# Gated GeGLU on one core: six units begin with the products that need no operand sums

## The chip, the cores and the metric

The kernel runs on one core of a Trainium2 chip. The metric is the device time of one execution in microseconds (us), as a median over runs. The core has a matrix engine (TensorE, PE in the profile), three elementwise engines (VectorE or DVE, ScalarE or ACT, GpSimd or POOL), a queue engine that issues the transfers here (SyncE or SP), and 16 DMA engines.

## What is computed

```python
# x (1, 2048, 1024), w_gate and w_up (1024, 3584), w_down (3584, 1024), all bf16
g = einsum("bsd,df->bsf", x, w_gate)
u = einsum("bsd,df->bsf", x, w_up)
h = gelu_tanh(g) * u
out = einsum("bsf,fd->bsd", h, w_down)
```

## The kernel before

All three products are done by the Strassen-Winograd scheme: a 2 by 2 block product takes seven block products instead of eight, at the price of sums of blocks, which the other engines make. The rows of x are taken in two passes of 1024, each as two chunks of 512 rows. A pass holds its rows transposed in two tiles `xT[0]` and `xT[1]`, each of eight K blocks of 128.

In the up projection a *unit* is 256 columns of w_gate and of w_up: two column blocks of 128, by two K halves of four blocks, against two row chunks. Its seven products, each four matmuls for gate and four for up, are P1 and P2, which use the bf16 blocks as loaded, and P6, P5, P3, P7, P4, which use sums in fp32r. The row sums `t1` to `t4` and the cast `tb` are made once per pass from `xT`; the weight sums `s1` to `s4` and the cast `sa` are made for each unit from its weight tile `w`. The first row chunk is `lo`/`hi` of `xT[0]`, the second of `xT[1]`.

P1 is copied out of PSUM by ACT (`snap`, the copy `p1`); P1 + P2 gives block (0,0) of the output. P6 is accumulated by the matrix engine onto P1 in the same PSUM bank; that sum is copied out as `u2`, and then P3 and later P4 are accumulated in the same bank again. P5 goes to another pair of banks, is copied out as `p5`, and P7 is accumulated on it.

The order on SP, DVE, POOL and PE, and in these sections on ACT, is the order in which the program is written (`manual_schedule`); nothing is reordered. All loads are issued by SP, one after the other.

The start is special. Four DMAs load the first 512 rows of x (`load_x`, L435), and PE transposes them, 32 blocks of 128 x 128, through four PSUM banks (`turn`, L444; seven and two dummy matmuls in `keep_warm`, L500, precede and separate them). The second 512 rows come transposed by DMA (`transposing`, L452), eight of them. The first 256 columns of the weights, unit 0, are done without the scheme: `plain` (L478) makes 32 bf16 matmuls for each row chunk, `finish` (L493) the gelu and the product with up. Between the two stand P1 and P2 of unit 1 (`raw_products`, L189). Then the units from 1 to 13 follow, called from L594 on. In an odd unit, ahead of P4, the raw products P1 and P2 of the next two units are done (`ahead_of_p4`, L584). `aside` (L576) makes t4 after P6 of unit 1 and loads the weights of the unit after next; `prepare` (L560) has POOL make the weight sums of the next unit. From unit 2 on, `keep_part` (L265) makes sums of w_down for the down projection in the same banks.

Tiles with the tag "k" (t, s, p1, u2, p5, g and others) share 52 slots of 2 KB per partition; weight tiles share three buffers of 8 KB.

Of the kernel before, what the change touches and what calls it, by code (L numbers as in the profile page):

```python
# [10 lines left out]
def kernel(  # L11
# [23 lines left out]
    nc = tc.nc  # L35
# [23 lines left out]
    NWARM = 7  # L59
    SLOTS = 52  # L60
# [44 lines left out]
    def snap(ps, name):  # L105
        t = slot([P, N], f32, name)
        nc.scalar.copy(out=t, in_=ps)  # L107
        return t

# [7 lines left out]
    def load_w(u, queue=nc.sync):  # L117
        f0 = u * 2 * P
        w = wpool.tile([P, 2, NKB, 2 * P], bf16, name="w")
        for i, src in enumerate((w_gate, w_up)):  # L120
            queue.dma_start(
                out=w[:, i],
                in_=src[:, f0 : f0 + 2 * P].rearrange("(ko ki) f -> ki ko f", ki=P),
            )
        return w

# [22 lines left out]
    def sums_s(w, eng):  # L149
        GU = range(2)  # L150
        sh = [P, KH, P]
        a11, a21 = [[w[:, i, :KH, h : h + P] for i in GU] for h in (0, P)]
        a12, a22 = [[w[:, i, KH:, h : h + P] for i in GU] for h in (0, P)]
        return Sums(
            how={
                "s1": lambda q, GU=GU: [new(eng, a21[i], a22[i], ADD, "s1", sh) for i in GU],
                "s2": lambda q: [new(eng, q["s1"][i], a11[i], SUB, "s2", sh) for i in GU],
                "s3": lambda q: [new(eng, a11[i], a21[i], SUB, "s3", sh) for i in GU],
                "s4": lambda q: [new(eng, a12[i], q["s2"][i], SUB, "s4", sh) for i in GU],
                "sa": lambda q: [cast(a22[i], "sa", sh) for i in GU],  # L160
            }
        )
# [26 lines left out]
    def raw_products(e, c, xT, w):  # L189
        for i in range(2):  # L190
            product(e[i], w[:, i, :KH, :P], [xT[0][:, k, :] for k in range(KH)], True)
        p1 = [snap(e[i], "p1") for i in range(2)]
        for i in range(2):
            b21 = [xT[0][:, KH + k, :] for k in range(KH)]
            product(c[i], w[:, i, KH:, :P], b21, True)
        return p1
# [6 lines left out]
    def finish_raw(u, c, p1):  # L203
        g, up = add(c, p1)
        times(2 * u, 0, gelu(g), up)

    def unit(u, banks, s, t, late, after_p5, aside, keep, ahead_of_p4, behind_p4):
        GU = range(2)
        e, c, d = banks
        aside(-2)  # L210
        g, up = late() if late else (None, None)
        aside(-1)
        for i in GU:
            product(e[i], s["s2"][i], t["t2"], False)
        aside(0)
        keep(0, c[0])
        u2 = [snap(e[i], "u2") for i in GU]
        if late:
            g = gelu(g)
        c11 = g, up  # L220
        keep(1, c[0])
        keep(2, c[1])
        c = d
        for i in GU:
            product(c[i], s["s1"][i], t["t1"], True)
        p5 = [snap(c[i], "p5") for i in GU]
# [3 lines left out]
        g, up = new(dve, e[0], p5[0], ADD, "sum", dtype=f32), banks[1][not late]  # L230
        dve(up, e[1], p5[1], ADD)
        if late:
            times(2 * u, 0, *c11)
        for i in GU:
            product(c[i], s["s4"][i], t["tb"], False)
        times(2 * u + 1, 1, gelu(g), up)
        aside(1)
        g, up = add(c, u2)
        times(2 * u, 1, gelu(g), up)
# [4 lines left out]
        times(2 * u + 1, 0, gelu(e[0]), e[1])  # L244
# [190 lines left out]
    def load_x(c):  # L435
        t = []
        for i in range(NS):
            xn = slot([P, Dm], bf16, "xn")
            r0 = c * N + i * P
            nc.sync.dma_start(out=xn, in_=x2[r0 : r0 + P, :])  # L440
            t.append(xn)
        return t

    def turn(xT, xn, c, i):  # L444
        tp = bank[4 + i].bitcast(bf16).rearrange("p (k r) -> p k r", k=NKB)
        for ko in range(NKB):
            nc.tensor.transpose(tp[:, ko, :], xn[i][:, ko * P : (ko + 1) * P], ident)  # L447
        for ks in (range(NKB),) if i < NS - 1 else (range(KH), range(KH, NKB)):
            ks = slice(ks.start, ks.stop)
            (on_act if i == 1 else on_dve)(out=xT[c][:, ks, i * P : (i + 1) * P], in_=tp[:, ks])  # L450
# [6 lines left out]
    def load_wf(queue, k0, k1):  # L457
        for i, src in enumerate((w_gate, w_up)):
            got = queue.dma_start(
                out=wf[:, i, k0:k1],  # L460
                in_=src[k0 * P : k1 * P, 0 : 2 * P].rearrange(
                    "(ko ki) f -> ki ko f", ki=P
                ),
            )
            if queue is not nc.sync:
                tc.keep_in_program_order(got)

    xT = new_x()
    xn0 = load_x(0)
    wf = wpool.tile([P, 2, NKB, 2 * P], bf16, name="w")  # L470
    for k0, k1 in ((0, 2), (2, 5), (5, NKB)):
        load_wf(nc.sync, k0, k1)
    w = load_w(1)
    for ko in range(NKB):
        transposing(xT, 1, ko, N)
    ahead = load_w(2)

    def plain(ps, c, kos, parts=1):  # L478
        n = N // parts
        for k in range(kos.start, kos.stop, 2):  # L480
            for part in range(parts):
                cols = slice(part * n, (part + 1) * n)
                for p, (j, i) in zip(ps, [(j, i) for j in range(2) for i in range(2)]):
                    for ko in (k, k + 1):
                        matmul(
                            p[:, cols],
                            wf[:, i, ko, j * P : (j + 1) * P],
                            xT[c][:, ko, cols],
                            ko == 0 and part == 0,
                            ko == NKB - 1,  # L490
                        )

    def finish(ps, c):  # L493
        for j in range(2):
            times(j, c, gelu(ps[2 * j]), ps[2 * j + 1])

    on_dve, on_act = nc.vector.tensor_copy, nc.scalar.copy
    s, t = sums_s(w, dve), sums_t(xT)
    with tc.manual_schedule(engines={ENG.Activation}):
        def keep_warm(n, cols):  # L500
            for _ in range(n):
                nc.tensor.matmul(
                    bank[3][:, :cols], lhsT=warm[:, :P], rhs=warm[:, :cols], start=True, stop=True
                )

        keep_warm(NWARM, N)
        for i in range(NS):
            if i == 2:
                keep_warm(2, 2 * P)
            turn(xT, xn0, 0, i)  # L510
        plain(bank[0:4], 0, range(0, 2), parts=2)
        plain(bank[0:4], 0, range(2, NKB))
        s["s3"] = sums_s(w, pool)["how"]["s3"](s)
        s["s1"] = s["how"]["s1"](s, range(1))
        finish(bank[0:4], 0)
        s["s1"] += s["how"]["s1"](s, range(1, 2))
        nxt = {"p1": raw_products(odd, cc, xT, w)}
        s.make("sa", "s2", "s4")
        t.make("t1")

    seen = xpool.tile([P, 1], f32, name="seen")

    def rest_of_0(part):
        if part == 0:
            plain(bank[4:8], 1, range(NKB))
            t.make("t2", "tb")
        else:
            t3 = t["how"]["t3"](t, range(0, 2))
            finish(bank[4:8], 1)
            t["t3"] = t3 + t["how"]["t3"](t, range(2, KH))  # L530
# [6 lines left out]
    E, K, C, F = odd, cc, dd, even  # L537

    def loaded(u):
        if u not in ws:  # L540
            ws[u] = load_w(u)
        return ws[u]

    def raw_of(u, e):
        p1 = raw_products(e, K, xT, loaded(u))
        return lambda: finish_raw(u, K, p1)

    for ip in range(NPASS):
        with tc.manual_schedule(engines={ENG.Activation}):
            if ip == 0:  # L550
                ws = {1: w, 2: ahead}
                late = lambda: add(cc, nxt["p1"])
            else:
                raw_of(0, F)()
                raw_of(1, C)()
            for u in range(1 if ip == 0 else 0, NU):
                js = making(u) if ip == 0 else []
                first = (ip, u) == (0, 1)

                def prepare():  # L560
                    if first:
                        pool_behind(t["t4"][-1])
                    if u + 1 < NU:
                        nxt["s"] = make_s(loaded(u + 1), pool)
# [11 lines left out]
                def aside(part):  # L576
                    if first and part < 0:
                        rest_of_0(part + 2)
                    if part == 0 and u + 2 < NU:
                        loaded(u + 2)  # L580
                    if part == 0 and "t4" not in t:
                        t.make("t4")

                def ahead_of_p4():  # L584
                    if u % 2 and u + 1 < NU:
# [7 lines left out]
                if u % 2 and not first:  # L593
# [3 lines left out]
                    u, banks, s, t, late if first else None, prepare, aside, keep,  # L597
                    ahead_of_p4, behind_p4,
# [6 lines left out]
        def more(step):  # L605
# [9 lines left out]
            if step == 50:  # L615
                ws.clear()
                ws.update({n: load_w(n) for n in range(2)})
            if step == 58:
                got["s"] = make_s(ws[0], dve)
# [36 lines left out]
```

## Time and profile before

| | |
|---|---|
| median of 3 runs | 540.39 us (540.03 to 541.08) |
| profiled execution: span from first to last instruction | 538.8 us |
| median of the runs less the span | 1.6 us |
| PE busy | 534.1 us, 99% of the span, 2409 matmuls |
| DVE, ACT, POOL busy | 341.5, 261.4, 238.5 us |
| moved by DMA | 93.29 MB, mean 173 GB/s |
| granted PE clock (mean) | 1.000 |

The profile gives the span of its own execution and no separate device time for it; the runs' median is 1.6 us above it. The chain that ended last is the list of what released what, followed back from the last instruction: 98% of it is PE. A timeline line has the start, the time from the first start to the last end of the merged instructions, the engine, the line of the program, the operation with its tiles, and how often. In a merged line the recorded ends overlap the next start, so a rate is read from start to next start. Start times are counted from the first instruction.

### The profile page before, as it was taken

The numbers are of one execution on the slowest core, as the hardware profiler recorded it, in microseconds if no ns is written. First come the engines' busy times: TensorE is split into PE (matmuls) and PEld (weight loads), VectorE is DVE, ScalarE is ACT, GpSimd is POOL, SyncE is SP. The second block draws the span as 40 slices with busy tenths as digits, with TensorE's granted clock in tenths as the row PEclk, the third lists the DMA queues.
The fourth block names the chain that finished last, engine by engine and source line by source line (L and its number), as shares of the span: only waits on it lengthen the run. The fifth ranks groups of instructions, "written<-read, shape, count | busy, mean of one in ns | idle before, by whom it ended". The sixth has DMA issues, their size and how long they took to land.

```text
span 538.8 us, 7447 instructions
## 1 busy us (share of the span) xinstructions
PE 534.1 (99%) x2409; PEld 381.2 (71%) x2409; DVE 341.5 (63%) x524; ACT 261.4 (49%) x463; POOL 238.5 (44%) x215
## 2 busy tenths in 40 slices
PE   8999999999999999999999999999999999999997
PEld 5568686867677746888867677676868685488886
DVE  2986766767676894694955455555554649676730
ACT  2556675766666410255355555555555551114431
POOL 1179966677773500000097767676766600000000
DMA  9675656749472999989872223242420049573751
GB/s 243 157 185 168 185 176 175 220 133 260 131 235 72 381 366 297 307 192 296 238 195 80 78 80 88 70 118 63 133 71 9 2 147 390 184 236 96 237 181 51
DMA packets 108198, 93.29 MB, mean 173 GB/s; under 512 B 17280, under 2 KB 93056, under 8 KB 108160
## 3 DMA queue, kind: packets, MB, share of 16 engines
q1 hardware_dynamic: 108160, 92.82, 59.4%
q8 instruction: 19, 0.31, 0.3%
q14 instruction: 19, 0.16, 0.1%
HBM read 74.45 MB, written 15.20 MB: 166 GB/s over the span
## 4 chain that ended last, share of the span: by engine, by line
PE 98%; DMA 1%; SPq 0%; ACT 0%; issue 0%
PE bank L111 98%; DMA xn<-in_x_dram 1%; SPq L440 0%; PE bank L447 0%; ACT st L412 0%
## 5 line engine op out<-in xcount | busy, mean ns | idle before, releaser
L93 POOL TENSOR_TENSOR s<-w 128x512 fp32r<-128x512 bf16 x102 | 119.2, 1189 | 163.2 <-DVE t L90 86.0
L111 PE MATMUL bank<-t,s 128*128 128x512 f32 x648 | 151.7, 390 | 0.0
L111 PEld LDWEIGHTS bank<-t,s 128*128 128x128 f32 x648 | 121.6, 188 | 25.5
L111 PE MATMUL bank<-xT,w 128*128 128x512 bf16 (+1 forms) x504 | 109.7, 376 | 0.0
L107 ACT COPY p<-bank 128x512 f32<-128x512 f32 x124 | 69.9, 590 | 45.4 <-PE bank L111 44.9
L111 PEld LDWEIGHTS <-w 128*128 128x128 bf16 x504 | 48.1, 98 | 58.1 <-issue 3.4
L90 DVE TENSOR_TENSOR hT<-g,bank 128x512 bf16<-128x512 f32 x112 | 76.8, 687 | 17.5 <-PE bank L111 4.5
L90 DVE TENSOR_TENSOR sum<-bank,p 128x512 f32<-128x512 f32 x54 | 37.3, 691 | 79.5 <-PE bank L111 78.4
L179 ACT ACTIVATE g<-sum 128x512 f32<-128x512 f32 x81 | 51.4, 635 | 74.5 <-DVE sum L90 74.2
L111 PE MATMUL bank<-q 128*128 128x512 f32 x240 | 58.9, 389 | 0.0
L93 POOL TENSOR_TENSOR s<-w,s 128x512 fp32r<-128x512 bf16 x50 | 57.7, 1176 | 0.0
L93 POOL TENSOR_TENSOR s<-s,w 128x512 fp32r<-128x512 f32 x50 | 57.2, 1165 | 0.0
L111 PE MATMUL bank<-t,sa 128*128 128x512 f32 x216 | 55.9, 401 | 0.0
L111 PE MATMUL bank<-tb,s 128*128 128x512 f32 x216 | 53.3, 389 | 0.0
L107 ACT COPY u<-bank 128x512 f32<-128x512 f32 x62 | 35.5, 589 | 33.5 <-PE bank L111 33.2
L111 PEld LDWEIGHTS bank<-q 128*128 128x128 f32 x240 | 45.0, 188 | 9.4
L111 PE MATMUL bank<-raw,hT 128*128 128x512 bf16 x224 | 48.7, 379 | 0.0
L102 ACT CAST tb<-raw 128x512 fp32r<-128x512 bf16 x28 | 17.3, 626 | 62.1 <-PE bank L111 27.6
L111 PEld LDWEIGHTS bank<-t,sa 128*128 128x128 f32 x216 | 40.6, 188 | 9.5
L111 PEld LDWEIGHTS bank<-tb,s 128*128 128x128 f32 x216 | 40.5, 188 | 8.4
L90 DVE TENSOR_TENSOR bank<-bank,p 128x512 f32<-128x512 f32 x54 | 37.7, 699 | 8.8 <-PE bank L111 6.2
L90 DVE TENSOR_TENSOR q<-hT 128x512 fp32r<-128x512 bf16 x56 | 38.4, 685 | 4.3 <-PE bank L111 4.3
(44 smaller groups left out, 442.1 us busy)
## 6 DMA issues: line engine op xcount, KB each, us to landing
raw<-in_w_down_dram SPq DMA_DIRECT2D x76, 256.0 KB, 5.0
q<-td SPq DMA_DIRECT2D x60, 256.0 KB, 5.1
w<-in_w_gate_dram SPq DMA_DIRECT2D x27, 512.0 KB, 5.9
w<-in_w_up_dram SPq DMA_DIRECT2D x27, 512.0 KB, 7.0
td<-m SPq DMA_DIRECT2D x12, 768.0 KB, 4.5
w<-td SPq DMA_DIRECT2D x6, 1024.0 KB, 10.0
out_dram<-st SPq DMA_DIRECT2D x32, 128.0 KB, 1.7
td<-w SPq DMA_DIRECT2D x2, 768.0 KB, 6.2
```

The costliest lines, as they stand in the source:

```text
L90: nc.vector.tensor_tensor(out=out, in0=a, in1=b, op=op)
L93: nc.gpsimd.tensor_tensor(out=out, in0=a, in1=b, op=op)
L102: nc.scalar.copy(out=t, in_=src)
L107: nc.scalar.copy(out=t, in_=ps)
L111: nc.tensor.matmul(ps, lhsT=lhs, rhs=rhs, start=start, stop=stop, skip_group_check=True)
L179: nc.scalar.activation(g, src, ACT.Gelu_apprx_tanh)
```

## The change

Unit 0 becomes a unit like the others, and units 0 to 5 begin with P1 and P2 (`early_p1`, `early_p2`), two units at a time in four bank pairs, before any of their sums is needed. Their P1 copies are kept: eight in slots, four in parts of `hT` that are not yet written. The other five products follow for each unit in turn. Since P1 is then no longer in the bank, P6 starts the bank afresh and DVE adds the kept P1 to it before ACT copies `u2`. The copies `u2` and `p5` of the first pass go into `xT[1]`, which is no longer read by then.

Column blocks are paired differently in units 0 to 5, so that P1 and P2 of two units need one weight tile only; weight tiles 3 to 5 are loaded into a part of `hT`. The first x chunk is loaded in two K halves of two DMAs each, between pieces of the first weight tile; PE transposes one half before P1 of units 0 and 1 and the other between their P1 and P2. From unit 6 on, and in the second pass, the work is as before.

The core of the diff (the new `load_w` takes a number, a tile and a K range; `turn` takes a half; `blocks_of` picks the column blocks):

```diff
-    def unit(u, banks, s, t, late, after_p5, aside, keep, ahead_of_p4, behind_p4):
+    def unit(fbs, banks, s, t, p1, spare, after_p5, aside, keep, ahead_of_p4, behind_p4):
...
         for i in GU:
-            product(e[i], s["s2"][i], t["t2"], False)
-        aside(0)
+            product(e[i], s["s2"][i], t["t2"], p1 is not None)
+        if p1:
+            for i in GU:
+                dve(e[i], e[i], p1[i], ADD)
+        aside()
         keep(0, c[0])
-        u2 = [snap(e[i], "u2") for i in GU]
...
+        u2 = [snap(e[i], "u2", spare[i]) for i in GU]
...
+    load_x(0)
+    load_w(0, wa[0], 0, 2)
+    load_w(0, wa[0], 2, 4)
+    load_x(1)
+    load_w(0, wa[0], 4, 6)
+    load_w(0, wa[0], 6, 8)
+    load_w(2, wa[2])
+    for ko in range(KH):
+        transposing(xT, 1, ko, N)
+    load_w(4, wa[4])
+    load_w(1, wa[1])
+    for ko in range(KH, NKB):
+        transposing(xT, 1, ko, N)
+    load_w(3, wa[3])
+    load_w(5, wa[5])
+    early = [blocks_of(wa[u // 2 * 2], wa[u // 2 * 2 + 1], u % 2) for u in range(R)]
...
+        for us in (((2, C), (3, F)), ((4, E), (5, K))):
+            for u, ps in us:
+                for i in range(2):
+                    early_p1(u, ps, i, range(KH))
+                early_snap(u, ps)
+            if us[0][0] == 2:
+                t.make("t1")
+                s_pool.make("s3")
+                s["s3"] = s_pool["s3"]
+                s.make("s1", "s2")
+            else:
+                t.make("t2", "t3", "tb")
+            for u, ps in us:
+                for i in range(2):
+                    early_p2(u, ps, i, range(KH))
+                early_c11(u, ps)
+        s.make("s4", "sa")
+        t.make("t4")
+        pool_behind(t["t3"][-1])
+        nxt = {"s": make_s(early[1], pool)}
```

`early_c11` is the gelu and the product with up for block (0,0) of a unit: one ACT and one DVE instruction.

## The prediction

> **What bounds the kernel now.** I read the page first (span, slices, chain), then the chain in order of time, then the timelines of PE, DVE and SP over the first 45 us, where the change lies. The page:
>
> ```profile
> span 538.8 us, 7447 instructions
> PE   8999999999999999999999999999999999999997
> DVE  2986766767676894694955455555554649676730
> DMA  9675656749472999989872223242420049573751
> PE 98%; DMA 1%; SPq 0%; ACT 0%; issue 0%
> ```
>
> PE is full in every slice but the first and last. DVE is near full only in the second slice (13.5 to 27 us), where the row sums are made. In the chain in order of time (start, length, what), what is left over is the load of x:
>
> ```profile
> 2.12 4.87 DMA xn<-in_x_dram
> ...
> 7.91 527.77 PE bank L111 x2366
> ```
>
> So a change pays by fewer PE microseconds after 7.9 us or by an earlier start, and any new PE wait is paid in full, since nothing later can take it back. PE's own timeline gives its rates:
>
> ```profile
> 7.49 17.66 PE L111 MATMUL bank<-xT,w 128*128 128x256 bf16 x88
> 24.80 5.84 PE L111 MATMUL bank<-t,s 128*128 128x512 f32 x24
> 30.48 1.98 PE L111 MATMUL bank<-tb,s 128*128 128x512 f32 x8
> 32.30 7.08 PE L111 MATMUL bank<-xT,w 128*128 128x512 bf16 x32
> 39.03 2.19 PE L111 MATMUL bank<-t,sa 128*128 128x512 f32 x8
> ```
>
> From start to start a bf16 product takes 0.216 us (the single records of these rows), an fp32r one 0.227: (32.30 - 24.80)/32 is 0.234 with the change of operands at its head. The first 88 records are 16 halves and 72 whole products: 80 in all. P3 of unit 1 begins 8 products before 30.48, at 28.66. That moment is my point of reference.
>
> **PE work.** Removed: 64 bf16 products of the plain unit. Added: one full unit, 16 bf16 and 40 fp32r. That is -48 x 0.216 + 40 x 0.227 = -10.4 + 9.1 = -1.3 us. Only eight products go, and cheap ones become dear ones. The transposes stay 32, but 16 of them (0.056 us each at full clock, 0.9 us) now stand in the middle of the products.
>
> **The start.** First products: x half 0 and the first pieces of the weights are 0.79 MB; before, the DMA that brought the sum to 0.79 MB landed at 6.26 us (trace of the landings), so I begin at about 6.2 instead of 7.5. P1 of units 0 and 1 (16 products) ends near 9.7; 16 transposes to 10.6; PE then waits for the last copy out of PSUM (0.69 us as in the DVE rows of the old copies, and some 0.2 behind it): 11.5. The remaining 80 early products take 17.3: P6 of unit 0 could begin at 28.8 and its P3 at 28.8 + 16 x 0.227 = 32.4. Per product done this is 0.5 us later than before (28.8 - 96 x 0.216 = 8.1 against 24.8 - 80 x 0.216 = 7.5). If nothing else waited, the sum would be -1.3 + 0.5 = -0.8 us.
>
> **The new wait.** Before, P6 was accumulated on P1 by PE, and the copy u2 needed no DVE; t4 was queued behind and cost nobody anything. Now u2 needs a DVE add, and in DVE's written order this add of unit 0 stands behind t1 (4 instructions), s1 and s2 (4), the products of units 2 and 3 (2), t2 (4), t3 (4), the products of 4 and 5 (2), s4 (2) and t4 (4). P3 cannot write the bank before u2 is out. DVE's rate:
>
> ```profile
> 12.39 0.69 DVE L90 TENSOR_TENSOR s<-w 128x512 fp32r<-128x512 bf16 x1 [3.94 <-DMA w<-in_w_gate_dram]
> ...
> 21.05 2.50 DVE L90 TENSOR_TENSOR t<-xT,t 128x512 fp32r<-128x512 bf16 x4
> 23.47 0.68 DVE L90 TENSOR_TENSOR sum<-bank,p 128x512 f32<-128x512 f32 x1
> ...
> 28.27 2.49 DVE L90 TENSOR_TENSOR t<-xT,t 128x512 fp32r<-128x512 bf16 x4
> ```
>
> Four take 2.42 us, 0.605 each; the first row also shows DVE standing 3.94 us for a weight load, with all behind it standing too. That returns: s1 of unit 0 needs weight tile 1, which SP now issues behind tiles 0, 2, four DMA transposes and tile 4. SP's timeline of before has the pieces:
>
> ```profile
> 7.06 1.60 SPq L121 DMA_DIRECT2D w<-in_w_up_dram  x1
> 8.71 12.73 SPq L453 DMA_TRANSPOSE xT<-in_x_dram  x8
> 21.48 0.58 SPq L121 DMA_DIRECT2D w<-in_w_gate_dram  x1
> 22.11 0.58 SPq L121 DMA_DIRECT2D w<-in_w_up_dram  x1
> 22.88 0.85 SPq L121 DMA_DIRECT2D w<-in_w_gate_dram  x1
> 23.77 1.56 SPq L121 DMA_DIRECT2D w<-in_w_up_dram  x1
> ```
>
> Ahead of the first transpose stand 14 DMAs instead of 12, with the same 3.1 MB: it goes out at about 9.05 instead of 8.71. The first took 2.64 us of SP to the next, the following 1.30 each: four take 6.5, so tile 4 is issued from 15.55. The four weight DMAs of the last rows landed at 25.56, 27.37, 29.18 and 30.96 (trace of the landings), the last 9.5 us after the first issue. So tile 1's gate half lands at 23.2 and its up half at L = 25.0. Bounds for L: not before 14.05 (where 3.1 MB had landed) + 0.5 MB of transposes + 2.1 MB at the rate of the row 22 to 31 us below + 0.8 of landing, 23.9; and 26.2 if tile 4 flows only after the fourth transpose has landed (18.19 before). I take 25.0, the same four DMAs behind the same kind of transposes.
>
> ```profile
> 16.00:22.00 6.00, 1.00 0.40 82
> 22.00:31.00 9.00, 1.00 1.06 273
> ```
>
> (window, its length, clock, DMA share, GB/s: transposes alone, then weights.) The transposes moved 82 GB/s, one per 1.3 us of SP. [...]
>
> From L on DVE has s1 of up, s2 (2), two products, t2, t3, two products, s4, t4: 21 instructions, 12.7 us, so the add of P1 begins at 37.75. It takes 0.69, the copy u2 0.59 (group of u copies), with 0.1 between: P3 begins at 39.15, not at 32.4. PE stands 6.7 us, of it 4.6 in one piece before P3: P5 of up must wait for the product of unit 4 to leave its bank (14th after L, done 33.6) and ends 34.55. The late hi transposes (issued 19.2 to 25.7, landing to about 28) are hidden: t2's last wants them at 29.9.
>
> **Sum.** After P3 of unit 0, PE has 40 fp32r more and 64 bf16 fewer than before after P3 of unit 1: 9.1 - 13.8 = -4.7 us. P3 comes 39.15 - 28.66 = 10.5 later. 10.5 - 4.7 = **+5.8 us**: span 544.6, time 540.4 + 5.8 = 546.2. The start no longer enters, since the path runs DMA, DVE, ACT, PE. L's bounds make it +4.7 to +7.0.
>
> **What I cost at nothing.** The other ten P1 adds: in units 1 to 5 DVE has 12 instructions (7.3 us) in a unit of 40 x 0.227 = 9.1 us, and the chain add 0.69 + copy 0.59 for gate starts when P6 of gate ends, 2.7 us before P3; uncovered it would be about 1.3 per unit. POOL makes 8 weight sums of about 1.12 per unit, 9.0 against 9.1: no room, but it starts behind t3 (32.9), has s2 of unit 1 at 37.6, and PE wants it at 44.6, so the stall itself buys 7 us of lead. Renumbered blocks, `spare` and the tiles in hT move no work; xT[1] is read for the last time by t3 and tb, before P5 is out.
>
> **The PE clock.** The profile shows products at half rate until 5.1 us (0.427 each for the dummies), and full rate kept over a pause of 0.8 us at 5.5. A pause of 4.6 us is not shown. Bounds: nothing, or another 4.3 us at half rate, 2.2 us lost; I take nothing, by the pause that is shown, and keep 2.2 for the range. [...]
>
> **Rivals.**
> - *The clock falls back in the pause*: 546.2 + 2.2 = 548.4. Chance 0.17.
> - *Not slower: DVE never waits for tile 1.* If its up half lands by 20.1 (so that 13 instructions end when P2 of unit 5 does, near 28), only the last product, s4, t4, the add and the copy follow the early products, 5.7 us against 3.6 of P6 and P5. P3 then comes at 34.5 with the start above: +1.1; with the first product at 5.6 (the copy, not the weights, ending last) and no pause before P2, 1.7 us sooner, -0.6. So 539.8 to 541.5. For it: only data and SP order, no engine, stand between. Against: 5.8 MB must have landed, and 273 GB/s and 1.3 us per transpose do not give that by 20. Chance 0.10.
> - *POOL and slots bound units 1 to 5.* If sums must wait for slots (POOL waited 28 us for PE and 24 for gelu later in the trace), POOL's 9.0 us per unit has nothing to catch up with; beyond the 7 us of lead, each us costs one. Up to +3: 549.2. Chance 0.08.
>
> **How the numbers follow.** The forecast has 0.62; 0.03 is left for what I do not see. Its own range is 545.1 to 547.4. The range of 8 in 10 goes from the not-slower case with the start above (541.5) to the upper L with half of the clock's loss and some of the slots' (549.6). About 0.2%, 1.1 us, is what can be told from no change. From the cases: faster 0.06, same 0.07, slower 0.87.
>
> **What would show it.** In the changed profile: DVE standing some 4 us ahead of s1 for `w`; u2's first copy waiting for a DVE add at about 38; PE with a pause of about 4.6 us ahead of P3 and one of 1 to 2 us in P6; the rest full. Wrong if the pause before P3 is under 2 us, or tile 1 lands by 20, or units 1 to 5 take more than 9.4 us each.

## The result and the profile after

The changed kernel takes 557.05 us (median of 5 runs, 556.65 to 557.80), the kernel before 540.21 in the same session: ratio 1.0313, 95% interval 1.0301 to 1.0326. It is slower, as forecast, but by 16.8 us and not by 5.8, and outside the range (541.5 to 549.6). The profiled span grew from 538.8 to 556.0 us.

The page of the changed kernel, the lines that answer to those shown of before, with the granted PE clock, which the page of before does not have:

```profile
span 556.0 us, 7452 instructions
PE   8956999999999999999999999999999999999997
DVE  1396787776776788478676546455455548866730
PEclk9986999999999999999999999999999999999999
DMA  9960059674846499999958242222222029662751
PE 89%; DVE 3%; SPq 3%; DMA 3%; issue 1%; ACT 0%; DVEq 0%; ACTq 0%
```

Nearly all of the damage is in slices 2 to 4 (14 to 56 us): PE falls to half full in the third, the clock is under 1 in the third and fourth, and the transfers stop in the fourth and fifth. From slice 5 on PE is full, as before. The chain (start, length, what) names the path:

```profile
19.00 7.93 DMA w<-in_w_up_dram
...
37.03 2.28 DVE s L91 x2
39.30 6.23 DVE t L91 x4
45.53 0.62 DVE bank L91
46.17 0.59 ACT xT L108
46.90 37.40 PE bank L115 x152
```

That is the forecast's chain, link by link: a late half of a weight tile, DVE's queue down to t4, the P1 add (`bank`), the copy u2 (written into `xT`), then PE. The sizes are what differs. DVE's timeline:

```profile
25.28 0.69 DVE L91 TENSOR_TENSOR s<-w 128x512 fp32r<-128x512 bf16 x1 [5.93 <-DMA w<-in_w_gate_dram]
26.96 0.69 DVE L91 TENSOR_TENSOR s<-w 128x512 fp32r<-128x512 bf16 x1 [0.99 <-DMA w<-in_w_up_dram]
...
33.35 2.48 DVE L91 TENSOR_TENSOR t<-xT 128x512 fp32r<-128x512 bf16 x4
35.75 1.27 DVE L91 TENSOR_TENSOR hT<-g,bank 128x512 bf16<-128x512 f32 x2
36.95 2.35 DVE L91 TENSOR_TENSOR s<-w,s 128x512 fp32r<-128x512 bf16 x2
39.23 6.30 DVE L91 TENSOR_TENSOR t<-xT,t 128x512 fp32r<-128x512 bf16 x4
45.45 1.28 DVE L91 TENSOR_TENSOR bank<-bank,p 128x512 f32<-128x512 f32 x2
```

Tile 1 was ready at 26.9, not 25.0. The 21 instructions took from 26.96 to 45.45, 18.5 us instead of 12.7. The four t3 (33.35) still take 0.6 each; the four t4 take 1.55 each, though they are the same kind of sum and took 0.6 in the kernel before. What else runs then is seen in POOL's timeline:

```profile
35.90 0.18 POOL L180 COPY seen<-t 128x1 f32<-128x1 f32 x1 [7.22 <-DVE t L91]
36.03 2.72 POOL L94 TENSOR_TENSOR s<-w 128x512 fp32r<-128x512 bf16 x2
38.72 3.15 POOL L94 TENSOR_TENSOR s<-s,w 128x512 fp32r<-128x512 f32 x2
41.84 3.15 POOL L94 TENSOR_TENSOR s<-w 128x512 fp32r<-128x512 bf16 x2
```

POOL is let loose behind t3 and works beside s4 and t4, at 1.56 us a sum from start to start, where it takes 1.12 alone (47.64 to 54.37). PE's timeline shows the rest:

```profile
31.67 6.03 PE L115 MATMUL bank<-t,s 128*128 128x512 f32 x16 [1.92 <-DVE t L91]
46.90 3.75 PE L115 MATMUL bank<-t,s 128*128 128x512 f32 x8 [9.20 <-ACT xT L108]
50.45 3.00 PE L115 MATMUL bank<-tb,s 128*128 128x512 f32 x8
53.29 1.99 PE L115 MATMUL bank<-t,sa 128*128 128x512 f32 x8
```

P3 begins at 46.90 after a pause of 9.20 us. From 46.90 to 50.45 eight products take 3.55 us, 0.44 each, and P7 another 2.84: half pace until 52.6. The windows of PE (window, its length, busy times, then granted clock, DMA share and GB/s) agree:

```profile
37.50:42.00 4.50, 0.20 (x1) 0.00 (x0) 4.50 (x4) 0.00 (x0) 4.50 (x4) 1.00 0.00 0
42.50:46.50 4.00, 0.00 (x0) 0.00 (x0) 4.00 (x4) 0.33 (x1) 4.00 (x3) 0.50 0.00 0
47.00:52.00 5.00, 5.00 (x12) 3.94 (x13) 1.84 (x3) 3.00 (x6) 5.00 (x5) 0.50 0.00 0
```

(The busy times are those of PE, PE's weight load, DVE, ACT and POOL.) PE stands while DVE and POOL are busy without a break, and the clock falls at 42.3. Last, in unit 5 P3 begins at 95.51 instead of 95.0 and P7 is 0.3 us longer: w_down arrives late.

The account against the forecast: late tile +1.95, slow DVE sums +5.8, clock +2.75 (6.39 us for P3 and P7 instead of 3.63), unit 5 +0.83 (from P6 to the products behind P7 it takes 8.31 us, and 7.48 in the run below without the late block). With the forecast's +5.75 this makes 17.1; the spans differ by 17.2.

### The profile page after: what moved, and what is told of

Same layout as the page of the kernel before. It is cut to its first block, busy times and chain, and to the rows that moved or that the text cites. A ratio compares the mean times of both kernels' runs of the same rounds, so it can differ in the third digit from the quotient of the medians.

```text
span 556.0 us, 7452 instructions
## 1 busy us (share of the span) xinstructions
PE 537.0 (97%) x2380; PEld 386.2 (69%) x2399; DVE 351.4 (63%) x530; ACT 265.5 (48%) x471; POOL 251.2 (45%) x223
## 4 chain that ended last, share of the span: by engine, by line
PE 89%; DVE 3%; SPq 3%; DMA 3%; issue 1%; ACT 0%; DVEq 0%; ACTq 0%
PE bank L115 89%; DVE t L91 2%; SPq L127 2%; DMA w<-in_w_up_dram 1%; SPq L476 1%; DMA raw<-in_w_down_dram 1%; DVE s L91 1%; DVE m L91 0%; DVE hT L91 0%; SPq L453 0%; ACT xT L108 0%; DVE bank L91 0%; ACT bank L281 0%; ACT st L422 0%; SPq L292 0%
## 5 line engine op out<-in xcount | busy, mean ns | idle before, releaser
L94 POOL TENSOR_TENSOR s<-w 128x512 fp32r<-128x512 bf16 x90 | 107.6, 1213 | 172.2 <-PE bank L115 100.2
L115 PE MATMUL bank<-t,s 128*128 128x512 f32 x672 | 161.4, 396 | 11.6 <-ACT xT L108 9.5
L115 PEld LDWEIGHTS bank<-t,s 128*128 128x128 f32 x672 | 127.8, 191 | 40.5 <-POOL s L94 10.4
L115 PE MATMUL bank<-xT,w 128*128 128x512 bf16 (+1 forms) x412 | 89.9, 375 | 2.2 <-DVE xT L470 1.0
L108 ACT COPY p<-bank 128x512 f32<-128x512 f32 x96 | 54.6, 590 | 46.3 <-PE bank L115 45.8
L115 PEld LDWEIGHTS <-w 128*128 128x128 bf16 x424 | 40.4, 98 | 50.1 <-issue 4.1
L91 DVE TENSOR_TENSOR sum<-bank,p 128x512 f32<-128x512 f32 x36 | 24.9, 692 | 75.9 <-PE bank L115 75.9
L115 PE MATMUL bank<-tb,s 128*128 128x512 f32 x224 | 56.4, 395 | 0.0
L103 ACT CAST tb<-raw 128x512 fp32r<-128x512 bf16 x28 | 17.3, 627 | 62.4 <-DMA raw<-in_w_down_dram 26.9
L115 PEld LDWEIGHTS <-hT 128*128 128x128 bf16 x256 | 24.8, 98 | 31.1 <-DMA hT<-in_w_up_dram 1.1
L108 ACT COPY xT<-bank 128x512 f32<-128x512 f32 x56 | 31.3, 589 | 23.3 <-DVE bank L91 18.1
```

Source lines behind the costliest of these rows:

```text
L91: nc.vector.tensor_tensor(out=out, in0=a, in1=b, op=op)
L94: nc.gpsimd.tensor_tensor(out=out, in0=a, in1=b, op=op)
L103: nc.scalar.copy(out=t, in_=src)
L115: nc.tensor.matmul(ps, lhsT=lhs, rhs=rhs, start=start, stop=stop, skip_group_check=True)
```

## Experiments

The theory after the result: (a) s4 and t4 are slow because POOL works beside them; (b) the P1 add stands behind them in DVE's queue; (c) the pause makes the clock fall; (d) all of it starts from the late tile. The rivals are named with each run. Five runs change one thing each in the changed kernel, four test the mechanisms in the kernel before, three combine.

**POOL later.**

```diff
-        pool_behind(t["t3"][-1])
+        pool_behind(t["t4"][-1])
```

> The changed kernel with one line different: GpSimd begins the weight sums of unit 1 behind the last t4 instead of the last t3. Theory (VectorE's sums of two SBUF operands run at half pace or less while GpSimd works): t4 falls from 6.2 to 2.4 us for four, s4 from 2.3 to 1.2 for two, P3 of unit 0 begins 4.9 us earlier (near 42.0), the pause before it is some 4.3 us, and the clock probably stays up: 557.0 - 4.9 - 2.75 = 549.4 (552.2 if the clock still falls). Rival (t4 and s4 are slow by their own operands): t4 stays at 6.2 us, time 557.0. Rival (GpSimd was needed early): t4 gets fast but P6 of unit 1 waits for s2, and the time moves by less than 2 us.

Measured 551.58 us, ratio to the kernel before 1.0212 (95% interval 1.0197 to 1.0228; so in brackets for every run). DVE's timeline:

```profile
36.78 1.28 DVE L91 TENSOR_TENSOR s<-w,s 128x512 fp32r<-128x512 bf16 x2
37.99 2.48 DVE L91 TENSOR_TENSOR t<-xT,t 128x512 fp32r<-128x512 bf16 x4
40.40 1.29 DVE L91 TENSOR_TENSOR bank<-bank,p 128x512 f32<-128x512 f32 x2
```

and PE's:

```profile
41.85 3.41 PE L115 MATMUL bank<-t,s 128*128 128x512 f32 x8 [4.33 <-POOL s L94]
```

With the same operands and POOL away, s4 and t4 are back at 0.6 each, and P3 begins 5.0 us earlier (4.9 expected). The pause of 4.3 us brought a lower clock too: P3 took 3.24 us from start to start (41.85 to 45.09), where eight products take 1.82 at 0.227 each, and the mean granted clock was 0.997. So the higher of the two expected times came. The release printed on the PE line is POOL's, but POOL's last sum for this product ended at 28.5; what came last is the copy u2. (a) holds.

**The add first.** s4 and t4 are made in `aside`, behind the P1 adds of unit 0:

```diff
-        s.make("s4", "sa")
-        t.make("t4")
+        s.make("sa")
...
                 def aside():
+                    if (ip, u) == (0, 0):
+                        s.make("s4")
+                        t.make("t4")
```

> The changed kernel with s4 and t4 of VectorE queued behind the two P1 adds of unit 0 instead of ahead of them. Theory (the adds stand in VectorE's queue behind t4): the adds begin at about 37.0 instead of 45.5, P3 of unit 0 at 38.5 instead of 46.9, no pause over 1 us there; but s4 and t4 then run beside GpSimd at 1.55 us each, P4 waits for the last t4 and for the sums behind it until about 48, and ends near 49 instead of 55.2: 551 us. Rival (the copy u2 waits for something else, a transfer or the bank): P3 still begins after 45, time 557.

Measured 552.59 us (1.0232, 1.0217 to 1.0247). PE's timeline:

```profile
31.19 8.81 PE L115 MATMUL bank<-t,s 128*128 128x512 f32 x24 [2.17 <-DVE t L91]
39.95 2.11 PE L115 MATMUL bank<-tb,s 128*128 128x512 f32 x8
46.86 3.57 PE L115 MATMUL bank<-t,sa 128*128 128x512 f32 x8 [4.79 <-DVE sum L91]
```

P6, P5 and P3 are one run of 24 products now: the pause before P3 is gone, so (b) holds. But t4 still took 6.2 us beside POOL, and the wait came back one step later, before P4: a wait that was moved, not removed. P4 ended at 50.26, 1.3 later than expected: its eight products took 3.40 us instead of 1.82, with a mean granted clock of 0.994 in this run, so the clock fell there too.

**The clock.** 36 matmuls on constants, into the unused first bank of the pair K, between P5 and P3 of unit 0:

```diff
+        idle = c[0]
...
+        for _ in range(36 if p1 is not None and fbs[0] == 0 else 0):
+            nc.tensor.matmul(idle, lhsT=warm[:, :P], rhs=warm, start=True, stop=True)
```

> The changed kernel with 36 dummy matmuls of 512 columns into an unused bank between P5 and P3 of unit 0, 7.8 us of work in a pause of 9.2. Theory (the PE clock halves because of the pause and costs 2.75 us behind it): granted clock 1.0 from 38 us on, P3 and P7 of unit 0 take 3.6 us together and not 6.4, 554.3 us. Rival (the clock loss lies beside other waits and costs nothing): clock up, time 557.

Measured 554.46 us (1.0267, 1.0244 to 1.0290). PE's timeline:

```profile
37.45 8.05 PE L241 MATMUL bank<-const-bfloat16-1.0 128*128 128x512 bf16 x36
46.83 2.08 PE L115 MATMUL bank<-t,s 128*128 128x512 f32 x8 [1.34 <-ACT xT L108]
48.87 2.12 PE L115 MATMUL bank<-tb,s 128*128 128x512 f32 x8
```

P3 begins at the same moment, but it and P7 take 4.0 us instead of 6.4, and the mean granted clock is 0.997 instead of 0.988. Work that computes nothing made the kernel 2.6 us faster. (c) holds, with its size.

**The order of the loads.**

```diff
-    load_w(4, wa[4])
     load_w(1, wa[1])
+    load_w(4, wa[4])
```

> The changed kernel with weight tile 1 loaded ahead of tile 4 instead of behind it. Theory (VectorE stands for tile 1, and all its later work with it): tile 1 lands near 23.4 instead of 26.9, tile 4 as much later; PE waits for tile 4 at about 22 but that lies beside VectorE's work; t2 is then held by the late row transposes (landing to 29.8), so VectorE gains 1 to 3 us: P3 of unit 0 at 44 to 46, 554 to 556 us. Rival (tile 1 is not what VectorE's chain starts from): no change or slower, since tile 4 is late for PE.

Measured 554.45 us (1.0273, 1.0253 to 1.0293). PE's timeline:

```profile
24.83 8.53 PE L115 MATMUL bank<-xT,hT 128*128 128x512 bf16 x32 [3.33 <-DMA hT<-in_w_gate_dram]
33.01 4.00 PE L115 MATMUL bank<-t,s 128*128 128x512 f32 x16
44.65 3.71 PE L115 MATMUL bank<-t,s 128*128 128x512 f32 x8 [7.65 <-ACT xT L108]
```

DVE had tile 1 at 23.0, 4.0 us sooner, but P3 gained only 2.25: t2 waited for the last row transpose, and the products of units 4 and 5 for tile 4. (d) holds in part: DVE's chain does start from tile 1, but the gain is cut by the next two transfers in the same queue, and with the tile 4.0 us sooner the time fell by 2.6 us only.

**Both of the first two.** The add first and POOL behind t4 (the two diffs above; the release of POOL and its sums of unit 1 are then written in `aside` too):

> The changed kernel with both of the first two edits: the P1 adds of unit 0 ahead of s4 and t4, and GpSimd behind t4. Theory: P3 of unit 0 at 38, s4 and t4 at 0.6 us each, done at 41.4, P4 at 42.5 without the pause, clock up; but GpSimd starts at 41.5 and has s2 of unit 1 only at 46.2, so P6 of unit 1 waits some 2 us for it and begins at 46.3 (55.2 in the changed kernel, 48.8 with the GpSimd edit alone): 548 to 549 us. Rival (both edits remove the same wait and add nothing together): 551.5.

Measured 547.81 us (1.0146, 1.0132 to 1.0160). PE's timeline:

```profile
42.83 2.14 PE L115 MATMUL bank<-t,sa 128*128 128x512 f32 x8 [0.18 <-DVE sum L91]
45.82 5.96 PE L115 MATMUL bank<-t,s 128*128 128x512 f32 x24 [0.85 <-POOL s L94]
```

Unit 0 runs through, and unit 1 waits for POOL, as expected, 0.85 us only since unit 0 ended late. The two edits together take 9.2 us off 557.05: what (a), (b) and (c) cost, less this new wait.

**w_down ahead of the store.**

```diff
+                    if ip == 0 and u < R:
+                        fetch_wd(making(u + 1))
                     if len(js) == 1:
                         store_made(js[0])
...
-                    if ip == 0:
+                    if ip == 0 and u >= R:
                         fetch_wd(making(u + 1))
```

> The changed kernel with the loads of w_down for the next unit queued on SP ahead of the store of the finished sums instead of behind it, in units 0 to 5. Theory (in unit 5 a block of w_down arrives late because SP issues it only after the store, and this costs 0.8 us): P3 of unit 5 begins 3.6 us after its P5, no wait of PE at 95 us, 556.2. Rival (the wait there has another cause): 557.0.

Measured 555.90 us (1.0293, 1.0279 to 1.0307), against 1.0301 to 1.0326 of the changed kernel: the intervals meet, so the time alone does not settle it. Its profiled execution also had tile 1 at 25.30, 1.7 us sooner, which this edit does not touch. In the trace P6, P5 and P3 of unit 5 are one run of 24 products without the gap. In the changed kernel ACT had stood there for w_down:

```profile
94.26 0.59 ACT L281 CAST bank<-raw 128x512 f32<-128x512 bf16 x1 [2.46 <-DMA raw<-in_w_down_dram]
```

With the loads ahead of the store ACT does not wait for w_down in units 2 to 5 at all, so the cause of the late block is shown. What it costs PE is not a fixed 0.5 us: in the other runs with the old order these 24 products took between 5.44 us (the run with dummies, no gap) and 6.15 (the changed kernel), and a difference of that size is below what the times of these runs tell apart.

**POOL beside t4 in the kernel before.** The reverse of the first edit, in the old kernel:

```diff
-                        pool_behind(t["t4"][-1])
+                        pool_behind(t["t3"][-1])
```

> The kernel before with one line different: GpSimd begins the sums of unit 2 behind the last t3 instead of the last t4, so that they run beside t4. Theory (two-SBUF-operand sums on VectorE run in step with GpSimd's): four t4 take 6.2 us instead of 2.5; P4 of unit 1 needs them only at 39.0, so most of it is hidden: 540.2 to 541.7 us, the rest through banks freed later. Rival (contention only with the changed kernel's operands): t4 stays at 2.5 us, time 540.2.

Measured 540.28 us (1.0008, 0.9998 to 1.0019). The expectation that t4 slows down fell: four t4 took 2.49 us, as in the kernel before. POOL's timeline shows why:

```profile
27.93 2.39 POOL L165 COPY seen<-t 128x1 f32<-128x1 f32 x1 [13.19 <-DVE t L90]
30.27 2.28 POOL L93 TENSOR_TENSOR s<-w 128x512 fp32r<-128x512 bf16 x2
```

The copy of a single column takes 0.18 us elsewhere; here it takes 2.39, until t4 is done (27.78 to 30.27). DVE went from t3 to t4 without a break, and POOL was held off. So the engine that waits need not be DVE. This is the profiled execution, 540.18 us; four of the eleven took 541.0 to 542.6, longer than any of the kernel before in that session (540.82 at most), and which engine waited in those was not profiled. In the changed kernel two products that read PSUM stand between t3 and s4; the refined theory is that POOL gets in there. Two runs test it.

> The kernel before with GpSimd's sums of unit 2 let loose behind the last t2 instead of the last t4, so that GpSimd gets in while VectorE is at an add on PSUM and then runs beside t3 and t4. Theory (two-SBUF-operand sums of the two engines take turns): t3 and t4 at 1.55 us each instead of 0.6, the last t3 at 32 instead of 28.3, P3 of unit 1 waits up to 2.7 us: 542.5 to 543.2. Rival (VectorE's sums in a row hold GpSimd off, as when it was let loose behind t3): t3 and t4 stay at 0.6, 540.2.

(The edit is the same line with `t["t2"]`.) Measured a median of 540.02 us (1.0034, 0.9998 to 1.0070), but three of its twelve timed executions took 547.0 to 547.5 and the other nine 539.7 to 540.3. In the three the mean granted clock was 0.994 to 0.997 and in the nine 1.0, so PE was below full clock for a while in the three. In the profiled one, of the nine, it went as the rival has it: POOL's weight tile came at 25.24, a sum got in beside a product of DVE, and the next sum was held off for 4.4 us while t3 and t4 ran at 0.6 each. That the three saw the other order is likely but not shown. The gap between t3 and t4, put there on purpose:

```diff
-            t3 = t["how"]["t3"](t, range(0, 2))
+            t.make("t3")
             finish(bank[4:8], 1)
-            t["t3"] = t3 + t["how"]["t3"](t, range(2, KH))
...
-                        pool_behind(t["t4"][-1])
+                        pool_behind(t["t3"][-1])
```

> The kernel before with GpSimd let loose behind the last t3, and VectorE's two products on PSUM moved from the middle of t3 to between t3 and t4, as the order is in the changed kernel. Theory (who has begun keeps the turn: GpSimd enters while VectorE reads PSUM, and from then on the two engines' SBUF sums alternate): four t4 take about 6.2 us instead of 2.5, with GpSimd's at 1.5 instead of 1.1; t4 ends at 34 instead of 30.7, which P4 does not need before 38.5, so the time stays within 540.2 to 542 (banks freed later). Rival (VectorE always holds GpSimd off in this kernel, and the slow t4 of the changed kernel comes from its operands): t4 at 2.5 us and GpSimd's first sum stretched over it, 540.2.

Measured 542.74 us (1.0043, 1.0030 to 1.0057), 0.7 above the expected end. DVE's timeline:

```profile
27.19 1.27 DVE L90 TENSOR_TENSOR hT<-g,bank 128x512 bf16<-128x512 f32 x2
28.38 5.51 DVE L90 TENSOR_TENSOR t<-xT,t 128x512 fp32r<-128x512 bf16 x4
```

and POOL's:

```profile
27.47 2.74 POOL L93 TENSOR_TENSOR s<-w 128x512 fp32r<-128x512 bf16 x2
30.17 3.18 POOL L93 TENSOR_TENSOR s<-s,w 128x512 fp32r<-128x512 f32 x2
```

With old operands, old loads and one break in DVE's run, t4 is slow: 5.44 us for four instead of 2.4. The late sums behind it held a bank for 1.85 us before P2 of unit 2. The run with POOL behind t3 differs from this one only in where the two products stand.

**The add alone.** In the kernel before, unit 1 only:

```diff
-            product(e[i], s["s2"][i], t["t2"], False)
+            product(e[i], s["s2"][i], t["t2"], late is not None)
+        if late:
+            for i in GU:
+                dve(e[i], e[i], nxt["p1"][i], ADD)
```

> The kernel before with only the new dependence of the change in unit 1: P6 starts its bank afresh, VectorE adds the kept P1 ahead of t4, and only then ACT copies u2. Theory (the add on the path costs what VectorE's queue ahead of it takes, not more): VectorE is at t3 until 28.3, the add ends 28.95, the copy 29.6, P3 begins at about 29.7 instead of 28.7: +1.0 us, 541.2. Rival (the add as such costs several us): 543 or more. Rival (hidden): 540.2.

Measured 541.40 us (1.0024, 1.0015 to 1.0033). P3 waited 0.90 us for u2. The new dependence by itself costs about 1 us (1.2 by the medians); it is DVE's queue ahead of it that makes it dear.

**Repairs together.** Tile 1 ahead of tile 4, the add first, the w_down loads first, and POOL in two parts:

```diff
+                s_next = sums_s(early[1], pool)
+                s_next.make("s1", "s2")
                 s.make("s1", "s2")
...
                         t.make("t4")
+                        pool_behind(t["t4"][-1])
+                        nxt["s"].make("s3", "sa", "s4")
```

> The changed kernel with four repairs: weight tile 1 loaded ahead of tile 4; the P1 adds of unit 0 ahead of s4 and t4; GpSimd makes s1 and s2 of unit 1 as soon as tile 1 is there and waits for the last t4 before s3 and s4; w_down loaded ahead of the store. Theory (late tile, queue order and shared access add up, nothing else): adds at 34.6 to 35.8, P3 of unit 0 at 36.6, P6 of unit 1 at 42.3, 543.8 us. Rival (GpSimd's early s1 and s2 take the time back from t2): P6 of unit 0 at 35 or later, 546.

Measured 545.12 us (1.0093, 1.0078 to 1.0108), 1.3 above what I expected. PE's timeline:

```profile
24.97 8.68 PE L115 MATMUL bank<-xT,hT 128*128 128x512 bf16 x32 [3.35 <-DMA hT<-in_w_gate_dram]
33.30 6.04 PE L115 MATMUL bank<-t,s 128*128 128x512 f32 x24
```

P6 of unit 0 began at 33.30, so the rival was wrong there, but s2 and t2 did slow beside POOL's early sums (s2 3.1 us for two, t2 4.25 for four), which delayed the adds by 1.2. What is left is mostly the wait of 3.35 for tile 4 and the lower clock behind it (8.3 us for 32 products, 6.9 at full pace; mean granted clock 0.997). The last run takes tile 4 out of SP's queue:

```diff
-    load_w(4, wa[4])
...
         early_snap(1, K)
+        load_w(4, wa[4], queue=nc.scalar)
```

> As the kernel with four repairs, but weight tile 4 is issued from ACT's queue behind the first four P1 copies, so that neither tile 1 nor the row transposes wait behind it. Theory (what is left of the loss is the wait for transfers): no wait for tile 4 at 21 us, t2 done at 27.5, P6 of unit 0 at 28.5, P3 at 32.3, P6 of unit 1 at 38.3: 539.8 us, no slower than the kernel before. Rival (the bytes, not the queue, set when tile 1 and the transposes land): P6 of unit 0 after 30.5, 542 us or more.

Measured 547.34 us (1.0135, 1.0121 to 1.0148): the rival was right. Nobody waited for tile 4 any more, but tile 1, though issued at 15.09 and 15.71 instead of 15.54 and 17.43, came at 24.7, 1.7 later than in the run before; and ACT, which issued the loads at 12.28 and 15.02, began the gelu of units 0 and 1 only at 16.8, so that DVE's t1 began 3 us late. The same bytes through a second queue were not faster here. None of these versions beats the kernel before.

## Why the prediction was wrong in size and right in kind

The chain was right: DVE stood 5.9 us for tile 1, u2 waited for the add at the end of DVE's queue, PE had its long pause ahead of P3, units 1 to 4 took 9.07 us each, and POOL was further ahead than claimed (s2 of unit 1 done at 41.9, wanted at 55.1). "The start no longer enters" was right too: the first products began at 5.8 instead of 7.5 and nothing came of it.

*Twenty-one instructions at 0.605.* This is the term that failed. I took DVE's pitch from rows in which POOL stood still, and only asked whether POOL would be in time, not what it did to DVE. POOL's s3 of unit 0 lay beside s2, and its sums of unit 1, released behind t3, beside s4 and t4: s2 took 2.2 us and s4 2.3, where two take 1.2 alone, and t4 6.2 where it takes 2.4. That is 5.9 more, and the whole took 18.5 instead of 12.7: the sum had the number of instructions right, and their pace beside POOL wrong. Releasing POOL behind t4 brought P3 forward by 5.0. What the two engines contend for is not shown; the runs show when it happened. Beside POOL's sums t4, with both operands in SBUF (the memory on the chip that holds the tiles), took 1.55 us a sum against 0.6 without; the P1 add (45.45), with one operand in PSUM, kept its 0.6 beside them; and POOL's copy took 2.39 against 0.18 where DVE was first. A pair of sums, one on each engine, took 1.55 us, less than 0.6 and 1.12 together, so here the two were not kept apart for the whole of both instructions.

*The clock at nothing.* I had a bound of 2.2 us and took the other end, by the shown pause of 0.8 us, which was far from 4.6. Behind the pause of 9.2 us it cost 2.75, and the dummies gave back 2.6; behind the pause of 4.3 us (POOL later) P3 and P7 took 5.1 us instead of 3.6, 1.5 lost, within the bound.

*Tile 1 at 25.0.* It was 26.9. I took the unhindered issue times of four weight DMAs. The first of them held SP for 1.96 us instead of 0.58, and in the kernel before the transpose in the same place, the fourth behind the long first one, held it for 2.27: the row was there, but I used the mean of the transposes. From 16.5 to 18.0 the transfers moved 8 GB/s, with tile 4 already issued. The hold is not fixed either: in the profiled execution of the w_down run it fell on the second DMA (1.82 us), 248 GB/s flowed from 17.0 on, and tile 1 was there at 25.3. What decides it is open. My bounds for L did not hold (26.9 against 26.2 at most), and the lower one was added up wrong: with the 273 GB/s of the row it is 24.4 and not 23.9. DVE is also near full in five slices of the page of before and not in the second alone; nothing in the sum rests on that.

*The rest at nothing* held, but for unit 5 (0.83 us): w_down is fetched behind a store in the same queue, and units that take 9.1 instead of 12.5 us on average probably leave it less room.

*The rivals.* "The clock falls back" happened, on top of the forecast. "DVE never waits for tile 1" did not: with tile 1 moved ahead, the transposes and tile 4 came late in its place. Nor did "POOL and slots bound units 1 to 5": units 1 to 4 took 9.07 us each.

## What to carry to other kernels

A step that is moved onto another engine's queue costs what is queued ahead of it (P3 waited 0.90 us with the add alone, in the old kernel, and 9.20 in the changed one, with s4 and t4 ahead of the add), at the pace that this queue has while the others work: look for the engine that works beside it (here POOL beside DVE) and ask whether both have sums of two SBUF operands at that time (t4 took 1.55 us a sum beside POOL and 0.6 without). Where two such runs must lie close, release the one engine behind the other's run (P3 came 5.0 us sooner), or keep that run unbroken: in the profiled runs of the old kernel four t4 took 2.49 us unbroken and 5.51 with two products on PSUM ahead of them, which let POOL in. And a pause of PE can be paid twice, here 9.2 us as a pause and 2.75 at half clock behind it.

## What the runs showed of the hardware that I had not expected

Which engine was held off changed with what stood between two runs of sums: in the old kernel, in the profiled runs, t4 took 2.49 us when it followed t3 directly and 5.51 when two products on PSUM stood between, with the same work on POOL. Once POOL was in, in the changed kernel, the two engines alternated, one sum each, 1.55 us on DVE and 1.56 on POOL.

The clock also fell behind a pause of only 1.9 us. In the changed kernel PE stood from 29.8 to 31.7 and was at half clock from 32.1 to 35.5 (window, its length, PE busy, clock, DMA share, GB/s):

```profile
29.00:30.00 1.00, 0.75 (x4) 1.00 0.36 76
30.00:31.00 1.00, 0.00 (x0) 1.00 0.89 211
31.00:32.00 1.00, 0.33 (x1) 1.00 1.07 313
33.00:34.00 1.00, 1.00 (x3) 0.50 1.11 271
```

In this kernel the two stretches at half clock were 3.4 us (32.1 to 35.5) and 10.2 us long (42.3 to 52.6). With tile 4 late, in the first run of the repairs, PE stood 3.35 us, and the mean granted clock of 0.997 comes to about 3.3 us at half clock (an estimate: 0.003 x 543.4 us / 0.5). The length of the pause alone probably does not decide: in the profiled run with POOL later PE stood for 2.1 us in the same place (up to 31.5), and its mean of 0.997 leaves room for about 3.3 us at half clock in all (0.003 x 549.3 us / 0.5, an estimate too), most of which P3 took behind the pause of 4.3 us: 1.4 us lost are 2.8 us at half clock. So the clock probably stayed up there behind the 2.1 us; the other three executions had 0.990 to 0.993. What decides is not shown.
